# Block-sparse attention and a hard-swish MLP in one kernel: the turning of the attention's output moved from TensorE to VectorE, with batch 0's first product in four parts

## The chip, the cores and the metric

One core of a Trainium2 chip runs the whole program. The metric is the device time of one execution in microseconds (us); the kernel before takes 340.51 us, the median of three runs (339.76 to 341.34).

## What is computed

Eight batches, eight heads, 32 global and 512 local tokens, head size 64. Global tokens attend to everything; local tokens attend to the global ones and to a band of 32 tokens to each side. The result, 4352 rows of 512, goes through a two-layer MLP with a hard-swish between.

```python
k_all = np.concatenate([k_g, k_l], axis=2); v_all = np.concatenate([v_g, v_l], axis=2)
out_g = sm(scale * q_g @ k_all^T) @ v_all
s_ll = np.where(abs(i - j) <= 32, scale * q_l @ k_l^T, -1e9)
out_l = sm(concat(scale * q_l @ k_g^T, s_ll)) @ concat(v_g, v_l)
x = concat(out_g, out_l).transpose(0, 2, 1, 3).reshape(4352, 512)
h = x @ w_in                      # 512 -> 2048
out = (h * np.clip(h + 3, 0, 6) / 6) @ w_out
```

## The kernel before

**Who sets the order.** The kernel does not emit instructions as it goes. It builds operations (`Op`) with an engine and a cost, puts them on named streams with ranks (L286), and `Plan.lay` (L118) lays them out on a clock of its own: at each step the operation that can start first, among those within 0.03 us the one of lowest rank. Operations that ScalarE (ACT) or VectorE (DVE) can do (`either`, L303, and a few others) go to the one that would end first, with `SPARE` added on DVE's side. Buffers (`Buf`) are claimed in the plan and freed at their last reader. What comes out is a fixed order of instructions for each engine; real waits come from the data. The planner's costs are its own, and no time in this text comes from them.

**Attention of a batch.** The 512 local tokens of a batch are 16 units of 32; unit i of the first half and unit i of the second half (f = 0, 1) are worked on together, and two such i make a pair, so four pairs (`local`, L603). A pair goes through scores on PE into the two s banks (L624 or, for batches 0 and 1, L637; in batch 0 every second pair takes m banks), masked maximum on DVE (L664), exponential on ACT (L670), turning on PE (L679), copy of the turned weights to `et` on ACT or DVE (L308, L310), values on PE into `a` (L693), and normalising on DVE (reciprocal L701, product L702) into `x`. Then `x`, which has tokens on partitions, has to be turned so that the model dimension lies on partitions: four 128x128 turns on PE into PSUM (L715) and a copy to `xt` (stream "xpc", L308 or L310). The global tokens (`globe`, L723, twice a batch) go the same way: scores L735 or L743, two maxima and their union (L751, L752), exponentials L757 and L758, turning L768, copy to `etg`, values L777, normalising L785 and L786, and one turn on PE (L792) with a copy to `xg`.

**MLP.** `moe_first` (L868) runs the first product in 16 groups (c), each four matmuls of 512 columns (L821) into one of three m banks; ACT makes min/relu's first half into `t` (L833), DVE multiplies (the gate, L828) into `gts`, and the m bank is free again. Batch 0 is done in two parts of 256 columns, so that it can start after two of the four pairs. `moe_second` (L885) takes 16 matmuls of 512 columns (L850) for each 128 tokens, also in m banks, then a copy to `ot` (L858 or L860) and one store from SyncE's queue (SP). The global tokens of all batches are done together near the end (`moe_global`, L891). The MLP of a batch runs on PE between the attention steps of the next; `hold` (L807) ties the attention of batch b to the progress of the first product of batch b − 1.

**Loads.** They go out on GpSimd's queue (POOL): q and k of batch 0, the global v, the four blocks of V (L470), then w_in in eight pieces, two halves of 1024 columns of four each (L498), of which at most three are on the way in the plan (`AHEAD`), then batch 1. A piece of w_in holds 64 partitions and two of the four 128-row blocks. Copies of the global v into the value tile `vs` ("spreads", L459) go out on SP, and the strips of local v are copied into `vs` by POOL, in batch 0 also by ACT and DVE (L484, L486). POOL also clears the second buffers (`clear`, L353).

Of the kernel before, what the change touches and what calls it, by code (L numbers as in the profile page):

```python
# [37 lines left out]
class Plan:  # L38
# [7 lines left out]
    SPARE, PHASES = 0.3, 9  # L46
# [137 lines left out]
def kernel(  # L184
# [13 lines left out]
    P = 128  # L198
# [19 lines left out]
    AHEAD = 3  # L218
# [23 lines left out]
    for c in range(NDFF):  # L242
        sizes[f"gts{c}"] = 2
# [42 lines left out]
    for name, rank in (("l0", 0), ("ld", 5), ("lq", -2), ("sh", 0), ("sq", 0), ("st", 2), ("g0", 0), ("ga", -9), ("first", -9), ("gc", -3), ("msk", 1), ("tq", lambda n: 0 if n < 5 else 3), ("kg", 0.5), ("vs", 1.5), ("clr", 1),  # L286
                       ("s", -1), ("mx", lambda n: 1.2 if n < 33 else 2.7), ("ex", 1.2), ("t", -0.5), ("etc", 0), ("av", 0), ("nm", 0),
                       ("xp", -1.2), ("xpc", 0), ("gx", 1), ("gxc", 1),
                       ("mf", lambda n: 9 + n * 1e-3), ("ms", lambda n: 9 + (n + 2 * NDFF + 2) * 1e-3), ("t1", 0), ("gate", -1.4), ("ot", 1.5)):
        plan.stream(name, rank)  # L290
# [161 lines left out]
    def vg_load(b, to):  # L452

        st = state[b]
        v = st["v"] = Buf("v", NI // 2 + 2)
# [3 lines left out]
        for u in (2, 3, 0, 1):  # L459
            a = ORDER[u].index("g") * W  # L460
            st["vs"][u, 0] = [load("sh", "SP", 0.5, 0.3, lambda u=u, a=a: vs[v.slot][a:a + W, u],
                                lambda: vg[v.slot][0:W].rearrange("p (j h) d -> p j h d", j=1).to_broadcast([W, NJ, H, D1]), [g], lat=2.0 + LATE[b])]
            st["vs"][u, 1] = list(st["vs"][u, 0])

    def v_loads(b, to):
# [7 lines left out]
        def shift(u, z, n, src, js, dj):  # L473
# [129 lines left out]
    def local(b, n, spare, halves=False):  # L603
# [8 lines left out]
        def scored(r):  # L612
            return mps[ps[r].slot] if spare else sps[r]
# [363 lines left out]
```

## Time and profile before

| | us |
|---|---|
| median of 3 runs (lowest, highest) | 340.51 (339.76, 341.34) |
| the profiled execution | 340.96 |
| its span, first to last instruction | 339.2 |
| TensorE clock granted, mean | 0.983 |
| ACT busy, of the span | 234.1 |
| POOL busy, of the span | 156.2 |

The profile page gives busy time by engine, the span in 40 slices with the busy share of each engine in tenths, the chain of work that ended last, followed back from the last instruction, and the costliest groups of instructions: line, engine, operation, output and inputs, count, then busy us, mean ns of one, and the idle time just before them with what ended it. PE is the matmul row of TensorE and PEld its weight loads. A timeline row gives start, length, engine, line and a count of merged instructions; the length of a matmul row holds the drain of its last matmul, so the price of a group on PE is read from the start of one row to the start of the next.

### The profile page before, as it was taken

How to read it: one execution, taken by the hardware profiler on the slowest of the kernel's cores; microseconds unless marked ns; L12 is line 12 of the kernel's file. 1: busy time of each engine (PE TensorE's matmuls, PEld its weight loads, DVE VectorE, ACT ScalarE, POOL GpSimd, SP SyncE). 2: the span in 40 equal slices, each digit the busy share in tenths (PEclk: the TensorE clock that was granted, in tenths of full speed). 3: DMA queues.
4: the chain of work that ended last, by engine and by line, in shares of the span. 5: the costliest groups of instructions: out<-in, count | busy, mean ns of one | idle time of the engine just before them, and what ended most of it. 6: DMA issues, size and time to landing. Idle time of an engine off the chain costs nothing.

```text
span 339.2 us, 11248 instructions
## 1 busy us (share of the span) xinstructions
PE 313.6 (92%) x4456; PEld 169.5 (50%) x4456; DVE 257.0 (76%) x952; ACT 234.1 (69%) x576; POOL 156.2 (46%) x195
## 2 busy tenths in 40 slices
PE   0648879899999999999999999999999999999996
PEld 0536656454455455544554555454545544445654
DVE  5887997678988799989998999899969844433310
ACT  4778778555888697679867784799699644443431
POOL 8899589108961982694359258756000000000000
PEclk9976999999999999999999999999999999999999
DMA  8989999979960996999679948991000000010103
GB/s 131 185 154 165 185 227 164 177 204 147 221 124 35 154 206 86 91 153 179 145 99 150 169 90 80 183 174 41 31 33 34 35 32 33 31 60 34 62 34 92
DMA packets 107076, 39.27 MB, mean 116 GB/s; under 512 B 92368, under 2 KB 100816, under 8 KB 107024
## 3 DMA queue, kind: packets, MB, share of 16 engines
q0 software_dynamic: 93536, 17.44, 64.6%
q1 hardware_dynamic: 12912, 20.99, 22.7%
q8 instruction: 35, 0.57, 0.7%
q10 hardware_dynamic: 576, 0.13, 0.2%
q14 instruction: 17, 0.14, 0.1%
HBM read 35.39 MB, written 8.91 MB: 131 GB/s over the span
## 4 chain that ended last, share of the span: by engine, by line
PE 87%; DVE 7%; issue 2%; POOL 1%; ACT 1%; POOLq 0%; ACTq 0%
PE m L850 36%; PE m L821 33%; PE t L679 5%; PE a L693 3%; PE s L624 2%; PE t L715 2%; DVE gts L828 1%; PE t L768 1%; PE s L735 1%; PE s L637 1%; PE a L777 1%; DVE sm L664 1%; POOL wout L298 1%; DVE kt L534 1%; DVE qt L529 1%
## 5 line engine op out<-in xcount | busy, mean ns | idle before, releaser
L850 PE MATMUL m<-wout,gts 128*128 128x512 f16 (+1 forms) x560 | 135.1, 373 | 0.0
L828 DVE SCALAR_TENSOR_TENSOR gts<-t,m 128x512 f16<-128x512 f32 (+1 forms) x160 | 95.2, 602 | 46.1 <-ACT t L833 45.0
L821 PE MATMUL m<-xt,win 128*128 128x512 f16 (+1 forms) x576 | 126.9, 359 | 3.0 <-DVE gts L828 1.9
L833 ACT ACTIVATE t<-m 128x512 f32<-128x512 f32 (+1 forms) x160 | 84.3, 532 | 44.6 <-PE m L821 41.2
L486 POOL COPY vs<-v 32x1056 f32<-32x1056 f32 (+3 forms) x81 | 78.2, 966 | 34.9 <-DMA v<-in_v_l_dram 30.1
L670 ACT ACTIVATE ex<-sm,mx 128x128 f16<-128x128 f32 x256 | 86.1, 394 | 8.4 <-DVE mx L664 7.9
L821 PEld LDWEIGHTS <-win 128*128 128x128 f16 x640 | 59.9, 99 | 54.3 <-issue 4.2
L850 PEld LDWEIGHTS <-gts 128*128 128x128 f16 x560 | 51.1, 98 | 48.5 <-issue 0.7
L664 DVE CUSTOM_DVE_ANT_0 sm<-s,mask 128x128 f32<-128x128 f32 x240 | 56.9, 285 | 5.9 <-PE s L624 2.9
L858 ACT COPY ot<-m 128x512 f32<-128x512 f32 (+1 forms) x34 | 19.5, 573 | 16.9 <-PE m L850 16.2
L298 POOL DMA_DIRECT2D rawq<-in_q_l_dram x12 | 12.6, 1057 | 36.2 <-DMA vs<-vg 16.3
L298 POOL DMA_DIRECT2D v<-in_v_l_dram x32 | 28.2, 905 | 0.0
L702 DVE TENSOR_TENSOR x<-a,rec 128x512 f16<-128x512 f32 x32 | 22.1, 692 | 1.1
L664 DVE DVE_READ_ACCUMULATOR2_ANT mx<- 128x1 f32 x256 | 21.3, 83 | 0.0
L679 PE MATMUL t<-ident,ex 128*128 128x128 f16 x256 | 20.9, 228 | 0.0
L679 PEld LDWEIGHTS <-ex 128*128 128x128 f16 x256 | 17.2, 102 | 5.5 <-issue 0.7
L637 PE MATMUL s<-kt,qt 32*32 32x128 f16 x384 | 7.0, 246 | 12.3 <-DVE kt L542 10.0
L571 DVE STREAM_TRANSPOSE qt<-rawq 128x512 f16<-128x512 f16 x24 | 15.9, 692 | 0.0
L575 DVE STREAM_TRANSPOSE kt<-rawk 128x512 f16<-128x512 f16 x24 | 15.8, 687 | 0.0
L308 ACT COPY et<-t 128x1024 f16<-128x1024 f16 x13 | 13.1, 1010 | 3.5 <-PE t L679 3.4
L637 PEld LDWEIGHTS <-qt 32*32 32x32 f16 x512 | 6.5, 102 | 17.7 <-issue 9.6
L310 DVE COPY et<-t 128x1024 f16<-128x1024 f16 x19 | 13.0, 685 | 3.0 <-PE a L693 2.6
(95 smaller groups left out, 262.7 us busy)
## 6 DMA issues: line engine op xcount, KB each, us to landing
out_dram<-ot SPq DMA_DIRECT2D x31, 256.0 KB, 2.1
vs<-vg SPq DMA_DIRECT2D x32, 132.0 KB, 5.8
v<-in_v_l_dram POOLq DMA_DIRECT2D x32, 128.0 KB, 6.5
rawq<-in_q_l_dram POOLq DMA_DIRECT2D x12, 256.0 KB, 5.8
rawk<-in_k_l_dram POOLq DMA_DIRECT2D x12, 256.0 KB, 7.2
rawq<-rawq SPq DMA_DIRECT2D x12, 254.0 KB, 5.6
rawk<-rawk SPq DMA_DIRECT2D x12, 254.0 KB, 5.7
win<-in_moe_w_in_dram POOLq DMA_DIRECT2D x8, 256.0 KB, 6.2
```

What stands on the lines that cost most here:

```text
L298: eng.dma_start(out=o() if callable(o) else o, in_=i() if callable(i) else i)
L486: (nc.gpsimd if op.engine == "POOL" else nc.vector).tensor_copy(out=o(), in_=i())
L637: nc.tensor.matmul(out=scored(r)[quarter(e ^ r, f), z:z + P], lhsT=pairs(qt[k.slot])[rows, c, i * W:(i + 1) * W, bb], rhs=pairs(kt[k.slot] ...
L664: nc.vector.tensor_tensor_reduce(out=sms[sm.slot], in0=scored(c // 2)[:, z:z + P], in1=masks[:, m, :], scale=-scale, scalar=3.0e38, op0=AL ...
L670: nc.scalar.activation(out=exs[ex.slot][:, un, c, :], in_=sms[sm.slot], func=EXP, scale=-1.0, bias=mxs[mx.slot])
L679: nc.tensor.matmul(out=turned(tp)[:, z:z + P], lhsT=exs[ex.slot][:, un, c, :], rhs=ident, is_transpose=True)
L702: nc.vector.tensor_tensor(out=xs[x.slot], in0=o[:, :, :, 0:D], in1=recs[rec.slot].to_broadcast([P, 2, NC, D]), op=ALU.mult)
L821: nc.tensor.matmul(out=o if len(x.shape) == 2 else o.rearrange("p (a c) -> p a c", a=2), lhsT=w_in_t[c // 8][:, m, (c % 8) * P:(c % 8 + 1) ...
L828: nc.vector.scalar_tensor_tensor(out=g, in0=shape(t1s[t1.slot][:, 0:n]), scalar=1.0, in1=shape(mps[ps.slot][:, 0:n]), op0=ALU.min, op1=ALU ...
L833: r = plan.add("t1", Op(("ACT", 0.09 + n * 0.00083), lambda: nc.scalar.activation(out=t1s[t1.slot][:, 0:n], in_=mps[ps.slot][:, 0:n], func ...
L850: nc.tensor.matmul(out=mps[ps.slot][:, 0:n], lhsT=gfn(c), rhs=w_out_t[c // 4][:, c % 4, cols], start=(c == 0), stop=(c == NDFF - 1))
L858: nc.scalar.copy(out=o, in_=i)
```

## The change

- `x` is turned by DVE: one instruction turns the sixteen 32x32 blocks of a 128-partition stretch in place and writes them to `xt`. So that 32x32 blocks are enough, the values are laid out another way: the four quarters of the partitions of `a` hold four heads and not two heads by two halves, so that a block's 32 columns are 32 of the 64 numbers of a head. The PE turn and the copy from PSUM go. Rows of w_in are loaded in the order that matches (four blocks of 32 rows to 128 partitions for each of the four m).
- The tokens in `xt` stand pair by pair, 128 columns a pair. So batch 0's first product can be done in four parts, a pair each, in the order 1, 0, 2, 3; four groups c share an m bank, one ACT instruction and one gate. The global tokens share two groups a bank. A stretch of 128 tokens in `gts` is now two stretches of 64 rows of the output, so a store becomes two.
- The global rows: both halves' values are one operation, with one normalising, and a turn on DVE; the two s banks are one tile, and one instruction takes the maximum over both.
- The planner: other ranks, `SPARE` 0.8 for 0.3, `AHEAD` 4 for 3, the first w_in load behind V's second block, and two of batch 0's four spreads behind V's third.

```diff
-    SPARE, PHASES = 0.3, 9
+    SPARE, PHASES = 0.8, 9
...
-    AHEAD = 3
+    AHEAD = 4
+    PARTS, CG = 4, 4
...
-    gts = [tiles(f"gts{r}_", NDFF, [P, Sl], FP16) for r in range(2)]
+    gts = [tiles(f"gts{r}_", NDFF // CG, [P, CG, Sl], FP16) for r in range(2)]
-    sps = tiles("s", 2, [P, 512], FP32, pp)
+    sps = tiles("s", 1, [P, 2, 512], FP32, pp)[0]
...
-                       ("s", -1), ..., ("ex", 1.2), ("t", -0.5), ("etc", 0), ("av", 0), ("nm", 0),
-                       ("xp", -1.2), ("xpc", 0), ("gx", 1), ("gxc", 1),
+                       ("s", -1), ..., ("ex", 1.2), ("t", -0.5), ("etc", -0.7), ("av", -1.5), ("nm", -1.5),
+                       ("xp", -0.5), ("gx", 1),
...
-        for u in (2, 3, 0, 1):
+        spread(b, (2, 3, 0, 1) if b else (2, 3), g)
...
+        if b == 0:
+            spread(b, (0, 1), vl[NJ - 2])
...
-        rows = moe_w_in.rearrange("(k a e d) c -> a k d e c", k=2, a=2, e=2)
+        rows = moe_w_in.rearrange("(k h a d) c -> k a h d c", k=2, h=4, a=2)
...
-                    got.append(load("l0", "POOL", 0.65, 1.4, w_in_t[i][a * D:(a + 1) * D, 2 * k:2 * k + 2],
-                                    rows[a, k, :, :, i * n:(i + 1) * n], got[-AHEAD:][:1] if len(got) >= AHEAD else ()))
+                    got.append(load("l0", "POOL", 0.65, 1.4, w_in_t[i][:, 2 * k + a], rows[k, a, :, :, i * n:(i + 1) * n],
+                                    got[-AHEAD:][:1] if len(got) >= AHEAD else state[0]["v0"][1:2] if not got else ()))
...
-                for c in range(NC):
-                    for e in range(2):
-                        for f in range(2):
-                            nc.tensor.matmul(out=o[quarter(e, f), un, c, 0:D + 1],
+                for f in range(2):
+                    for kh in range(2):
+                        for hq in range(4):
+                            h = 4 * kh + hq
+                            c, e = h // 2, h % 2
+                            nc.tensor.matmul(out=o[hq * W:(hq + 1) * W, f, 2 * un + kh, 0:D + 1],
...
         def xturn():
-            o = turned(xp)[:, 0:4 * P].rearrange("d (k z n q) -> d k z n q", k=2, z=NU, n=2)
-            for un in range(2):
-                for kk in range(2):
-                    nc.tensor.matmul(out=o[:, kk, :, un, :], lhsT=xs[x.slot][:, un, 2 * kk:2 * kk + 2].rearrange("p a d -> p (a d)"),
-                                     rhs=ident, is_transpose=True)
-        a = plan.add("xp", Op(("PE", 0.24), xturn, done, [xp], [x], lat=0.25, n=8))
-        st["xT", n] = either("xpc", ...)
+            nc.vector.transpose(out=xts[xt.slot][:, :, n * P:(n + 1) * P].rearrange("p k (t q) -> p t k q", q=W),
+                                in_=xs[x.slot].rearrange("p f (u k) (a q) -> p (f u) (k a) q", u=2, a=2))
+        st["xT", n] = plan.add("xp", Op(("DVE", 0.7), xturn, done, new, [x]))
...
-            for f in range(2):
-                nc.vector.tensor_reduce(out=tops[mx.slot][:, f:f + 1], in_=sps[f][:, 0:N1]..., axis=AX, op=ALU.max)
+            nc.vector.tensor_reduce(out=tops[mx.slot][:, 0:1], in_=sps[:, :, 0:N1], axis=AX, op=ALU.max)
...
+        a = plan.add("av", Op(("PE", 0.48), lambda: [f(av) for f, _, _ in both], ...))
+        st["xg"] = plan.add("gx", Op(("DVE", 0.22), lambda: nc.vector.transpose(
+            out=xg[:, :, b * Sg:(b + 1) * Sg], in_=xgns[xgn.slot].rearrange("p k (a q) -> p (k a) q", q=W)), [n], (), [xgn]))
...
-        parts = 2 if b == 0 else 1
+        parts = PARTS if b == 0 else 1
+        for at, h in enumerate((1, 0, 2, 3) if parts == 4 else range(parts)):
+            for c in range(0, NDFF, parts):
+                cs = range(c, c + parts)
...
-               [(out[row:row + P, :], 0, P)], parts)
+               [(rows[f, j * P // 2:(j + 1) * P // 2], f * P // 2, P // 2) for f in range(2)], parts)
```

More of the change, by code (lines that the diff above doesn't have):

```diff
@@ L241 @@
              "eg": 2, "etg": 2, "xgn": 2, "t1": 3, "ot": 3, "m": 3, "t": 1, "s": 1, "a": 1, "mx": 16, "rec": 4}
-    for c in range(NDFF):
+    for c in range(NDFF // CG):
         sizes[f"gts{c}"] = 2
@@ L741, in scores @@
                     for cc, e, z in four:
-                        rows, c = quarter(e, f), 2 * cc + s
-                        nc.tensor.matmul(out=sps[f][z, 0:N1], lhsT=pairs(qg[k.slot])[rows, c, :, bb],
+                        rows, c = quarter(e, f), 2 * cc + of(cc)
+                        nc.tensor.matmul(out=sps[z, f, 0:N1], lhsT=pairs(qg[k.slot])[rows, c, :, bb],
                                          rhs=pairs(kt[k.slot])[rows, c, 2 * W:2 * W + N1, bb], start=(bb == 0), stop=(bb == 1))
@@ L784, in normal @@
[L784 to L796 removed]
+                    q = 2 * of(cc) + e
@@ L899, in moe_global @@
         for i in range(B // per):
-            second(lambda c, i=i: gts[gb[c].slot][c][:, i * P:(i + 1) * P], lambda c: [gb[c]], lambda c: [gd[c]],
+            second(lambda c, i=i: gts[gb[c].slot][c // CG][:, c % CG, i * P:(i + 1) * P], lambda c: [gb[c]], lambda c: [gd[c]],
                    [(rows[i * per + b, 0:Sg, :], b * Sg, Sg) for b in range(per)])
@@ L934 @@
                 globe(b, s)
+            globe_values(b)
         for b in range(B):
             moe_first(b)
-            for j in range(NJ - (b == B - 1)):
+            for j in ((1, 0, 2, 3) if b == 0 and PARTS == 4 else range(NJ - (b == B - 1))):
                 moe_second(b, j)
```

135 lines of the change are left out of this document (68 added, 67 removed).

## The prediction

> **What bounds the kernel now.** I read the page's busy shares and slices first, then its chain of work that ended last.
>
> ```profile
> span 339.2 us, 11248 instructions
> PE 313.6 (92%) x4456; PEld 169.5 (50%) x4456; DVE 257.0 (76%) x952; ACT 234.1 (69%) x576; POOL 156.2 (46%) x195
> ...
> PE   0648879899999999999999999999999999999996
> ...
> DVE  5887997678988799989998999899969844433310
> ...
> PE 87%; DVE 7%; issue 2%; POOL 1%; ACT 1%; POOLq 0%; ACTq 0%
> ```
>
> The reader is to see three stages. In slices 1 to 8 of 8.5 us PE has holes and DVE has 5 to 9 tenths; from slice 9 PE is full almost to the end; DVE has 9 tenths in most slices up to the 31st and falls off from the 33rd. A busy PE is a modelled PE, so the second look is at stretches, at PE's waits and at the chain inside the full stretch (three answers below: busy time by stretch; PE's waits from 21 to 76 us, then the same question for 76 to 330 us, which has its heading and no row; the chain from 76 to 326 us).
>
> ```profile
> 21.00:48.50 27.50, 21.62 (x391) 15.79 (x380) 24.30 (x92) 20.93 (x60) 22.31 (x30) 0.82 1.25 180
> 76.00:270.00 194.00, 194.00 (x2868) 98.36 (x2867) 176.42 (x665) 153.69 (x370) 103.95 (x111) 1.00 0.97 117
> ...
> PE m L821 <- DVE gts L828: 1.9, 2, 1.4
> ...
> engine line waited for: us in total, times, longest us
> ...
> by line: PE m L821 41.9%; PE m L850 39.7%; PE t L679 4.6%; PE a L693 3.4%; PE s L624 3.3%; PE t L715 2.2%; PE s L735 1.7%; PE t L768 1.5%; PE a L777 1.4%; PE t L792 0.2%; issue 0.0%
> ```
>
> In a stretch the columns after its length are the busy us of PE, PEld, DVE, ACT, POOL. From 76 to 326 us the chain is PE alone and PE waits for nobody: there, PE work taken away is time taken away, as long as DVE (176.4 of 194 us, 91%) and ACT (79%) still keep ahead. From 21 to 48.5 us DVE is busy 24.3 of 27.5 us and PE 21.6: there DVE sets the pace, and PE work there is nearly free.
>
> **The change part by part.**
>
> **The turning of x on PE, L715 and L792, goes.** PE's timeline gives its price as displacement, start to start, not as busy time:
>
> ```profile
> 67.80 0.40 PE L715 MATMUL t<-ident,x 128*128 128x128 f16 x4
> ...
> 73.14 0.39 PE L715 MATMUL t<-ident,x 128*128 128x128 f16 x4
> ...
> 121.87 0.61 PE L679 MATMUL t<-ident,ex 128*128 128x128 f16 x8
> 122.32 1.89 PE L821 MATMUL m<-xt,win 128*128 128x512 f16 x8
> 124.14 0.43 PE L693 MATMUL a<-vs,et 128*32 128x65 f16 x32
> ...
> 124.85 1.90 PE L821 MATMUL m<-xt,win 128*128 128x512 f16 x8
> 126.58 0.39 PE L715 MATMUL t<-ident,x 128*128 128x128 f16 x4
> 126.81 1.89 PE L821 MATMUL m<-xt,win 128*128 128x512 f16 x8
> ...
> 150.28 0.22 PE L792 MATMUL t<-ident,xgn 128*128 128x128 f16 x1
> 150.34 1.89 PE L821 MATMUL m<-xt,win 128*128 128x512 f16 x8
> ```
>
> A pair's turn takes 126.81 − 126.58 = 0.23 us of PE. The chain says the same: 2.2% of 250 us is 5.5 us for the 24 pairs of batches 2 to 7. With batch 1's four (67.8 to 73.5 us, PE full too) it is 28 × 0.23 = 6.4 us. Batch 0's four lie where DVE rules; I take nothing for them. The global rows' turn is 150.34 − 150.28 = 0.06 us, 8 times: 0.5 us.
>
> **The two value sums of the global rows become one.** One change of PE's array shape fewer per batch. Its price is the hole ahead of a group of that shape: eight products of 512 columns take 126.58 − 124.85 = 1.73 us, those at 122.32 are done at 124.05, and the value group starts at 124.14, so 0.09 us; eight of them, 0.7 us. Bounds 0 and 8 × 0.43 (the busy time of a whole value group) = 3.4 us; I take the hole, since all 80 matmuls stay.
>
> **DVE and ACT exchange work.** DVE gets 32 block transposes of 128x512 and 8 of 128x128. In the order that the planner lays out for the changed kernel it loses 18 of 19 copies of et, all 11 of xt, both of etg and xg, and its gates and maxima come in fewer, longer instructions. Rows of the groups by shape:
>
> ```profile
> L571 DVE STREAM_TRANSPOSE qt<-rawq 128x512 f16<-128x512 f16 x24 | 15.9, 692 | 0.0
> L578 DVE STREAM_TRANSPOSE qg<-gn 128x128 f16<-128x128 f16 x6 | 1.7, 284 | 0.0
> L310 DVE COPY et<-t 128x1024 f16<-128x1024 f16 x19 | 13.0, 685 | 3.0 <-PE a L693 2.6 <-PE t L679 0.2
> L310 DVE COPY xt<-t 128x512 f16<-128x512 f16 x11 | 4.6, 423 | 3.0 <-PE t L715 2.9
> L828 DVE SCALAR_TENSOR_TENSOR gts<-t,m 128x512 f16<-128x512 f32 x112 | 76.2, 682 | 30.4 <-ACT t L833 29.5
> L828 DVE SCALAR_TENSOR_TENSOR gts<-t,m 128x256 f16<-128x256 f32 x48 | 19.0, 416 | 15.8 <-ACT t L833 15.4
> L751 DVE TENSOR_REDUCE top<-s 128x1 f32<-128x288 f32 x32 | 12.9, 445 | 0.9 <-PE s L735 0.9
> L786 DVE TENSOR_TENSOR xgn<-a,rec 128x64 f16<-128x64 f32 x16 | 3.6, 225 | 0.6
> L308 ACT COPY et<-t 128x1024 f16<-128x1024 f16 x13 | 13.1, 1010 | 3.5 <-PE t L679 3.4
> L308 ACT COPY xt<-t 128x512 f16<-128x512 f16 x19 | 11.1, 582 | 6.2 <-PE t L715 6.1
> L833 ACT ACTIVATE t<-m 128x512 f32<-128x512 f32 x112 | 66.6, 595 | 30.3 <-PE m L821 27.7 <-PE t L715 0.8 <-DVE gts L828 0.7
> L833 ACT ACTIVATE t<-m 128x256 f32<-128x256 f32 x48 | 17.7, 384 | 14.3 <-PE m L821 13.6 <-DVE xgn L786 0.2
> ```
>
> DVE gains 32 × 0.69 + 8 × 0.28 = 24.4 us. It loses 18 × 0.685 + 11 × 0.42 = 17.0 us of copies; 48 × 0.416 − 24 × 0.682 = 3.6 us of gates; 2.3 us of maxima (32 of 288 columns become 16 of 576, at 0.445 + 288 × (0.682 − 0.416)/256 = 0.74 us each, 14.2 − 11.9); and half of L786, 1.8 us: 24.7 us, the few copies of etg and xg not counted. So DVE stays as it is. ACT loses 21 × 0.58 = 12.2 us of xt and 48 × 0.384 − 24 × 0.595 = 4.2 us of L833 and gains 18 × 1.01 = 18.2 us of et: 2 us more. The PE-bound stretch shrinks from 194 to about 187 us: DVE goes from 91 to about 94% there, ACT from 79 to some 84%. I cost the exchange at nothing; the cover is that slack, and the second and third rivals are its loss. The bound downward is nothing too, since PE already waits for neither.
>
> **Batch 0's first product in four parts.** 128 matmuls of 256 columns become 256 of 128 columns, each with a weight load of its own. Eight turns of 128 columns, also with a load each, take 122.32 − 121.87 = 0.45 us, 56 ns each; eight of 512 take the 1.73 us, so 108 ns for 256 columns. Hence 256 × 56 − 128 × 108 ns = +0.5 us, which I take. Bounds: 0 (pure columns), and 256 × 99 − 128 × 108 ns = +11.5 us if each waited out its weight load (the L821 PEld row below); the eight turns speak against that end. By the Trainium skill (TensorE: Matmul & The Clock Gate, section "Back-to-back issue gap") a sustained stream of loads and 128-column matmuls runs at about 81 ns each, which would make it +6.9 us; this trace's 56 ns does not agree.
>
> **The start.** The first product can begin when one pair is turned, not two, and the four loads of w_in's first half are issued together, after the clearing that used to follow them on POOL, 12.51 to 15.83 us, 3.3 us.
>
> ```profile
> 27.75 2.72 PE L821 MATMUL m<-xt,win 128*128 128x256 f16 x12
> ...
> 10.75 1.83 POOL L298 DMA_DIRECT2D win<-in_moe_w_in_dram  x3
> 12.51 0.62 POOL L354 MEMSET vg<- 128x528 f16 x1
> ...
> 15.30 0.53 POOL L361 MEMSET vs<- 32x528 f16 x1
> ...
> 20.52 0.59 POOL L298 DMA_DIRECT2D win<-in_moe_w_in_dram  x1
> ...
> win<-in_moe_w_in_dram POOLq DMA_DIRECT2D x1, 256.0 KB, 3.7
> ...
> L821 PEld LDWEIGHTS <-win 128*128 128x128 f16 x640 | 59.9, 99 | 54.3 <-issue 4.2
> ...
> 61.24 0.38 SPq L298 DMA_DIRECT2D out_dram<-ot  x1
> ```
>
> Issued from 10.75 + 3.3 = 14.1 us on, about 0.6 us each, they are out by 16.5 us, where the fourth used to go out at 20.5 and land 3.7 us later at 24.2. So the first product should start near 24 to 25 us, not 27.75. That is not the gain, because DVE rules until 48.5 us. In the new order DVE has, up to batch 1's first maxima, two copies of et and one of xt less, four transposes more, and 12 gates of 512 in place of 20 of 256: 4 × 0.69 + 12 × 0.682 − 2 × 0.685 − 0.42 − 20 × 0.416 = 0.8 us more, but 24 half-size gates' worth done in place of 20, which are 4 × 0.416 = 1.7 us ahead: 0.9 us gained. DVE's idle time, 27.5 − 24.3 = 3.2 us, may shrink besides, between nothing and all of it; of that I take a third, since the products now come in more and earlier pieces. Below nothing: the next half of w_in is the first rival. I take 2.0 us, bounds −2.6 and 4.1. That w_in waits for V's second block and two spreads for its third moves only the planner's clock: SP's queue begins in the same order as before, so nothing for it.
>
> **The stores** become two of 64 rows in place of one of 128. An issue takes SP 0.38 us (61.24 us); SP has long gaps, and what is queued behind, the spreads and the doubled q and k of the next batches, is needed a batch later. Only the last part's second issue is on the path: −0.3 us, between 0 and −0.4. The changed ranks and the V buffer's earlier release only shape the order counted above.
>
> Sum: 6.4 + 0.5 + 0.7 + 2.0 − 0.5 − 0.3 = 8.8 us off the profiled execution's own 340.96 us (its span 339.2 and 1.8 around it): 332.2. That execution is 0.4 us over the median of 340.51, so I say 332.0.
>
> **The rivals.**
> - **w_in's second half comes late.** Its loads follow six V copies on POOL, at about 21 to 24 us, and the new order has its first use as the third group of the first quarter, at about 28 us, with the global rows' scores behind it on PE (in the kernel before it was the ninth group). A load's form changes from 64 rows of two pieces to four blocks of 32 rows. If that form spread over a quarter of the DMA engines, the 3.7 us alone would become up to 14.8; halfway, about 9, the last lands near 33, PE stands 5 us, DVE's own work covers half of it, and the start loses 2.6 in place of gaining 2.0: 336.8. For it: four loads at once hide such a form, one after another does not. Against: no row shows a load spread less. The Trainium skill (DMA: Bandwidth & Descriptors, section "Why a DMA increments its semaphore by 16 and not by 1") has a rule of this kind: the number of engines is the largest up to 16 that divides the slowest dimension of both sides, here 4; no run here shows it yet.
> - **PE's freed time turns into waits on DVE at 94%.** Then only the start and the small terms remain: 340.96 − 2 = 339. For it: the 9 tenths of DVE in most slices; against it: PE waited for nothing in those.
> - **Slower: the three m banks.** Place: L821's groups, which need a bank back from L833 and L828. While two other groups run (2 × 0.86 = 1.7 us), 0.595 + 0.682 and some 0.1 of gaps must pass: 0.35 us to spare. An et copy of 1.01 us on ACT ahead of L833 overshoots by 0.66 us; the 18 copies that move there would cost 11.9 us: 332.2 + 11.9 = 344. It decides from about 9 us, where it eats the gain, so from three quarters of the copies standing there. Against: 13 et and 19 xt copies are on ACT now and PE waits for none; and second-product groups lie between for half the time.
> - **Better:** every term at its good bound: 4.1 for the start, nothing for the 128-column products and the stores, 3.4 for the value groups: 332.2 − 2.1 − 0.8 − 2.7 = 326.6.
>
> **How the numbers follow.** Forecast 332 (328.5 to 335) 0.62; late w_in 0.14; waits on DVE 0.09; slower 0.09; better 0.06. The range 327 to 338 holds the forecast and late w_in, and leaves out the slower case, most of the waits on DVE and the far end of the better one. About 0.5%, 1.7 us, is what a measurement of this kernel can tell from no change: faster 0.62 + 0.14 + 0.06 and a third of the waits on DVE, 0.85; within it the other two thirds, 0.06; slower 0.09.
>
> **What would show it.** PE's waits from 76 us on still empty, no L715 or L792 rows, and the first product's groups 0.23 us closer together; DVE's total within 5 us of 257 and ACT's of 234; new transposes near 0.69 us; 16 matmuls of 128 columns about 0.9 us apart; the first product near 24 to 25 us. Wrong if PE shows waits on L828 or L833 in the full stretch, if w_in's loads land 8 us or more after issue, or if the 128-column groups take over 1.2 us.

## The result, and the profile after

| | before | after |
|---|---|---|
| median of the runs (16 and 16, same chip) | 340.93 us | 336.91 us |
| lowest to highest | 339.44 to 342.04 | 336.20 to 340.17 |
| profiled execution, its span | 340.96, 339.2 | 336.76, 335.0 |

The ratio is 0.9893, 95% interval 0.9876 to 0.9909: faster by 4.0 us, 1.1%. The forecast was 332.0, which is 8.5 us under the 340.51 known then, so less than half of the forecast gain came; the time itself lies at the first rival's 336.8. Of the experiments below, one execution each of e7_spare03 and e8_old_order was slow and is left out, which lowers their medians by 0.3 us.

Busy shares, three of the slice rows and the summary of the chain, from the page of the kernel after:

```profile
span 335.0 us, 11129 instructions
PE 306.6 (92%) x4448; PEld 164.8 (49%) x4448; DVE 255.5 (76%) x902; ACT 239.2 (71%) x548; POOL 155.7 (46%) x193
...
PE   0547978899999999999999999999999999999994
...
DVE  5886697678878988998998899889988986442210
...
PE 85%; POOL 4%; DVE 3%; DMA 3%; issue 2%; ACT 1%; POOLq 0%; ACTq 0%
```

PE lost 7.0 us of busy time (313.6 to 306.6). DVE's total stayed (257.0 to 255.5) and ACT's grew by 5.1. New in the chain is DMA with 3%, one piece of 11 us.

The steady part, by the busy time of one stretch (after its length: PE, PEld, DVE, ACT, POOL), by PE's waits from 76 to 330 us (the heading has no row under it) and by the chain from 76 to 326 us:

```profile
76.00:270.00 194.00, 193.90 (x2734) 94.51 (x2732) 175.67 (x642) 158.58 (x362) 104.17 (x111) 1.00 1.03 121
...
engine line waited for: us in total, times, longest us
...
by line: PE m L828 42.6%; PE m L855 41.1%; PE t L688 4.3%; PE a L705 3.4%; PE s L633 3.4%; PE s L742 1.6%; PE t L773 1.4%; PE a L783 1.2%; DVE top L757 0.3%; DVE xt L725 0.3%; issue 0.3%; DVE rec L713 0.1%; DVE x L714 0.0%; DVE mx L758 0.0%
```

PE is still the bound and waits for nobody, and L715 and L792 are gone from its chain. The chain now touches DVE for 0.7%, some 1.7 us, most of it near 112 us; in two of the experiments PE waits for DVE just behind that place. To see what that is worth, the kernel is cut at two instructions that both versions have: batch 1's first product of 512 columns, and ACT's last copy, which starts as PE ends. From the timelines of PE and ACT (start, length, what), first before:

```profile
74.87 1.89 PE L821 MATMUL m<-xt,win 128*128 128x512 f16 x8
...
336.07 0.37 ACT L858 COPY ot<-m 128x256 f32<-128x256 f32 x1 [1.33 <-PE m L850]
```

and after:

```profile
75.81 1.89 PE L828 MATMUL m<-xt,win 128*128 128x512 f16 x8
...
330.53 0.37 ACT L863 COPY ot<-m 128x256 f32<-128x256 f32 x1 [1.37 <-PE m L855]
```

| stage | before | after | change | forecast |
|---|---|---|---|---|
| to batch 1's first 512-column product | 74.87 | 75.81 | +0.94 | 2.0 + 0.9 − 0.5 = 2.4 earlier |
| from there to ACT's last copy | 261.20 | 254.72 | −6.48 | 24 × 0.23 + 7 × (0.06 + 0.09) = 6.6 less |
| from there to the end of the span | 3.1 | 4.5 | +1.3 | +0.3 |

The steady part came as forecast to a tenth, which is in part luck: the steady parts of three other kernels with PE's old work (e2_before_newform, e9_before_order, e10_before_spare) took 260.1 to 261.2 us. Of the missing 4.6 us (8.8 forecast for this execution, 4.2 got) 3.4 are in the start and 1.0 in the tail.

In the start, rows from the timelines of PE and of its weight loads, and the loads' median from issue to landing, after:

```profile
25.48 0.51 PE L828 MATMUL m<-xt,win 128*128 128x128 f16 x2
26.45 3.03 PE L828 MATMUL m<-xt,win 128*128 128x128 f16 x26 [0.46 <-DMA win<-in_moe_w_in_dram]
...
33.50 0.64 PE L828 MATMUL m<-xt,win 128*128 128x128 f16 x4
...
33.90 0.10 PEld L828 LDWEIGHTS <-win 128*128 128x128 f16 x1 [0.25 <-DMA win<-in_moe_w_in_dram]
...
win<-in_moe_w_in_dram POOLq DMA_DIRECT2D x8, 256.0 KB, 10.6
```

The first product starts at 25.48 us, 2.3 earlier than before, and stops for 0.46 us after two matmuls, for w_in's first half. The third group, which needs w_in's second half, comes at 33.50, and its last weight load waits 0.25 us for it. PE's waits from 21 to 76 us hold no other wait for w_in. A load of w_in lands 10.6 us after its issue; before, the same row said 6.2. The chain from 21 to 50 us and POOL's timeline say what that held up:

```profile
by line: DMA win<-in_moe_w_in_dram 38.0%; PE m L828 23.8%; DVE gts L835 12.0%; DVE qt L538 6.8%; DVE kt L543 6.7%; ACT ex L679 5.4%; issue 3.7%; PE t L688 3.0%; DVE x L714 2.4%; PE t L773 2.2%; DVE xt L725 2.1%; PE s L750 2.1%; PE a L705 2.
...
15.38 11.02 DMA win<-in_moe_w_in_dram
...
29.56 0.87 POOL L299 DMA_DIRECT2D v<-in_v_l_dram  x1 [1.22 <-DMA win<-in_moe_w_in_dram]
32.24 0.87 POOL L299 DMA_DIRECT2D v<-in_v_l_dram  x1 [1.80 <-DMA win<-in_moe_w_in_dram]
33.60 0.87 POOL L299 DMA_DIRECT2D v<-in_v_l_dram  x1 [0.49 <-DMA win<-in_moe_w_in_dram]
```

The piece of 11 us is the load that completes w_in's first half, from its issue to its landing at 26.40. It stands on the chain because the products behind it start when it lands. And three of batch 1's four V loads wait on POOL, 3.5 us in all, each until a load of w_in has landed; before, the four went out in one run at 29.32.

In the tail, the last stores in SP's queue. Before:

```profile
336.47 0.35 SPq L298 DMA_DIRECT2D out_dram<-ot  x1
```

after:

```profile
330.74 1.87 SPq L299 DMA_DIRECT2D out_dram<-ot  x3
...
332.02 0.59 SPq L299 DMA_DIRECT2D out_dram<-ot  x1
```

Before, the last store went out at 336.47, as ACT's last copy ended (336.07 + 0.37). After, that copy ends at 330.90 and the last store goes out at 332.02: SP issues the last three back to back, 1.87 us for three, and the last one's data had been there for 1.1 us.

### The profile page after: what moved, and what is told of

It is laid out like the page before. It is cut to its first block, busy times and chain, and to the rows that moved or that the text cites. A ratio compares the mean times of both kernels' runs of the same rounds, so it can differ in the third digit from the quotient of the medians.

```text
span 335.0 us, 11129 instructions
## 1 busy us (share of the span) xinstructions
PE 306.6 (92%) x4448; PEld 164.8 (49%) x4448; DVE 255.5 (76%) x902; ACT 239.2 (71%) x548; POOL 155.7 (46%) x193
## 4 chain that ended last, share of the span: by engine, by line
PE 85%; POOL 4%; DVE 3%; DMA 3%; issue 2%; ACT 1%; POOLq 0%; ACTq 0%
PE m L855 35%; PE m L828 35%; PE t L688 4%; DMA win<-in_moe_w_in_dram 3%; PE a L705 3%; PE s L633 3%; PE t L773 1%; PE s L742 1%; POOL v L299 1%; DVE gts L835 1%; PE s L646 1%; POOL wout L299 1%; PE a L783 1%; DVE qt L538 1%; DVE kt L543 1%
## 5 line engine op out<-in xcount | busy, mean ns | idle before, releaser
L855 PE MATMUL m<-wout,gts 128*128 128x512 f16 (+1 forms) x560 | 132.1, 374 | 0.0
L828 PE MATMUL m<-xt,win 128*128 128x512 f16 (+1 forms) x704 | 124.9, 327 | 3.2 <-DVE gts L835 2.5
L835 DVE SCALAR_TENSOR_TENSOR gts<-t,m 128x512 f16<-128x512 f32 x136 | 91.7, 682 | 35.7 <-ACT t L839 34.2
L839 ACT ACTIVATE t<-m 128x512 f32<-128x512 f32 x136 | 80.9, 596 | 45.8 <-PE m L828 43.5
L828 PEld LDWEIGHTS <-win 128*128 128x128 f16 x768 | 65.2, 101 | 56.1 <-issue 4.6
L309 ACT COPY et<-t 128x1024 f16<-128x1024 f16 x29 | 29.3, 1009 | 7.3 <-PE t L688 7.2
L725 DVE STREAM_TRANSPOSE xt<-x 128x512 f16<-128x512 f16 x32 | 22.5, 704 | 0.2
L705 PEld LDWEIGHTS <-et 128*32 128x32 f16 x1024 | 10.2, 98 | 13.9 <-ACT ex L679 5.1
L309 ACT COPY etg<-t 128x640 f16<-128x640 f16 x16 | 11.1, 691 | 8.2 <-PE t L773 8.2
L705 PE MATMUL a<-vs,et 128*32 128x65 f16 x1024 | 14.4, 198 | 2.5 <-issue 1.2
## 6 DMA issues: line engine op xcount, KB each, us to landing
win<-in_moe_w_in_dram POOLq DMA_DIRECT2D x8, 256.0 KB, 10.6
```

The lines of the kernel that those rows point to most:

```text
L309: nc.scalar.copy(out=o(), in_=i())
L705: nc.tensor.matmul(out=o[hq * W:(hq + 1) * W, f, 2 * un + kh, 0:D + 1], lhsT=ets[et.slot][:, un, c, quarter(e, f) if b >= WORDS else quart ...
L725: nc.vector.transpose(out=xts[xt.slot][:, :, n * P:(n + 1) * P].rearrange("p k (t q) -> p t k q", q=W), in_=xs[x.slot].rearrange("p f (u k ...
L828: nc.tensor.matmul(out=mps[ps.slot][:, k * n:(k + 1) * n], lhsT=w_in_t[c // 8][:, m, (c % 8) * P:(c % 8 + 1) * P], rhs=x, start=(m == 0), ...
L835: nc.vector.scalar_tensor_tensor(out=g, in0=shape(t1s[t1.slot][:, 0:all_]), scalar=1.0, in1=shape(mps[ps.slot][:, 0:all_]), op0=ALU.min, o ...
L839: r = plan.add("t1", Op(("ACT", 0.09 + all_ * 0.00083), lambda: nc.scalar.activation(out=t1s[t1.slot][:, 0:all_], in_=mps[ps.slot][:, 0:al ...
```

## The experiments

Every kernel ran beside the kernel before on the same chip (medians of that: 341.06 us in the first and third group of runs, 341.2 in the second). Medians and ratios to it; the text compares medians, which the ratios bear out to within 0.9 us:

| run | us | ratio, 95% interval |
|---|---|---|
| e1_oldform | 334.20 | 0.9788 [0.9758, 0.9818] |
| e2_before_newform | 342.60 | 1.0042 [1.0017, 1.0068] |
| e3_parts2 | 338.47 | 0.9913 [0.9879, 0.9948] |
| e4_tail | 336.05 | 0.9850 [0.9817, 0.9882] |
| e5_heads | 334.53 | 0.9799 [0.9775, 0.9823] |
| e6_heads_tail | 333.96 | 0.9787 [0.9761, 0.9813] |
| e7_spare03 | 341.21 | 1.0006 [0.9982, 1.0031] |
| e8_old_order | 338.87 | 0.9929 [0.9905, 0.9953] |
| e9_before_order | 342.35 | 1.0032 [1.0004, 1.0059] |
| e10_before_spare | 344.38 | 1.0085 [1.0052, 1.0118] |
| e11_turns | 340.03 | 0.9958 [0.9932, 0.9984] |

**The loads' form, taken back in the kernel after.** The same eight loads of 256 KB in the same places of every queue, but in the form of the kernel before:

```diff
-        rows = moe_w_in.rearrange("(k h a d) c -> k a h d c", k=2, h=4, a=2)
+        rows = moe_w_in.rearrange("(k a e d) c -> a k d e c", k=2, a=2, e=2)
...
-   w_in_t[i][:, 2 * k + a], rows[k, a, :, :, i * n:(i + 1) * n]
+   w_in_t[i][a * D:(a + 1) * D, 2 * k:2 * k + 2], rows[a, k, :, :, i * n:(i + 1) * n]
```

> The changed kernel, with w_in's eight loads in the form of the kernel before (64 partitions, two blocks of rows each); the same places, sizes and order of every instruction. Rows of w_in then stand in an order that does not match x, so the output is another product; nothing else differs. Theory A (the start is lost to the loads' new form, which lands in 10.6 us in place of 6.2): landing falls to 7 us or less, the third group of the first product starts at 31 us or earlier in place of 33.5, and the time falls by 1.5 to 3 us below the changed kernel's 336.9, to some 334.5. Theory B (the start is lost to the order on PE and ACT and to PE's half clock): landing may fall, the time stays within 0.7 us of 336.9.

334.20 us, 2.7 under the kernel after; its slowest execution (334.82) lies under the fastest of the kernel after (336.20). PE's timeline and the landing:

```profile
25.59 2.83 PE L828 MATMUL m<-xt,win 128*128 128x128 f16 x28
...
32.27 0.40 PE L828 MATMUL m<-xt,win 128*128 128x128 f16 x4
...
72.41 1.89 PE L828 MATMUL m<-xt,win 128*128 128x512 f16 x8
...
win<-in_moe_w_in_dram POOLq DMA_DIRECT2D x8, 256.0 KB, 6.0
```

The loads land in 6.0 us, the first 28 matmuls run without a stop, and batch 1's first product is at 72.41 us: 2.5 earlier than in the kernel before, against 2.4 forecast. Nothing but the form of the loads was changed, so the form costs the 2.7 us.

The stages of this pair overstate it, since PE's granted clock differs: from 34 to 38 us it was 0.57 in the kernel after and 1.00 here, and the same 16 short products took 1.84 us there (35.24 to 37.08) and 0.99 here (33.59 to 34.58). That theory B's clock is not the cause of the rest is shown by e5_heads below.

**The new form alone, in the kernel before.**

```diff
-        rows = moe_w_in.rearrange("(k a e d) c -> a k d e c", k=2, a=2, e=2)
+        rows = moe_w_in.rearrange("(k h a d) c -> k a h d c", k=2, h=4, a=2)
```

> The kernel before, with w_in's eight loads in the changed kernel's form (128 partitions in four blocks of 32 rows), three on the way as before. Rows of w_in then do not match x, so the output is another product. Theory A: landing rises from 6.2 to about 10 us, the first product starts at 29 us or later in place of 27.75, and the time rises by 1 to 4 us. Theory B: within 0.7 us of the kernel before.

342.60 us, 1.5 over the kernel before. The landing goes from 6.2 to 10.2 us and the first product from 27.75 to 30.57, 2.8 later; by batch 1's first 512-column product 0.8 of it is left (75.68 against 74.87). So the new form costs time in both kernels, here about half of what it costs in the kernel after. Why the kernel after is hit harder was not tried apart; that it needs w_in's second half in the third group and not in the ninth can be little of it, since only the 0.25 us above were waited for.

**Two parts in place of four.**

```diff
-    PARTS, CG = 4, 4
+    PARTS, CG = 2, 4
```

> The changed kernel with batch 0's first product in two parts of 256 columns again (two groups a bank), all else as changed; the planner lays out a somewhat other order at the start. Theory C (in four parts, the first product's matmuls run at PE's half clock ahead of the turning of pair 2 and push pairs 2 and 3 back): turning of pair 2 moves from 29.3 to about 27 us and the time falls by 1 to 2 us. Theory A: the loads still land late, the time stays within 0.7 us or rises, since a first product of 256 columns must wait for two pairs.

338.47 us, 1.6 over the kernel after, though the intervals of the two ratios overlap. The first product comes at 28.61 us instead of 25.48, after a wait of 0.89 us for the second pair's turning. Theory A holds: the short matmuls were not what the kernel after lost, and the four parts are worth something between nothing and 1.5 us.

**Every second store of the tail from ACT.**

```diff
-            for o, p0, rows in stores:
-                load("st", "SP", 0.4, ...)
+            for at, (o, p0, rows) in enumerate(stores):
+                late = at % 2 and (parts == 2 or len(stores) == 4)
+                load("sa" if late else "st", "ACT" if late else "SP", 0.4, ...)
```

> The changed kernel with every second store of the global rows and of the last two half tiles issued from ACT's queue, which is nearly idle there, in place of SP's. Theory D (the doubled stores queue up on SP at the end: the last one goes out at 332.0 us where its data are ready at 330.9): the end comes 0.8 to 1.3 us earlier, 335.8, and the last landing is 3.2 us or less after PE's end in place of 4.5. Rival: the store's landing itself got longer, then less than 0.4 us changes.

336.05 us, 0.9 under the kernel after; as with the two parts, the intervals overlap, so the stage has to decide. From ACT's timeline:

```profile
330.38 0.37 ACT L863 COPY ot<-m 128x256 f32<-128x256 f32 x1 [0.66 <-PE m L855]
330.78 0.50 ACTq L299 DMA_DIRECT2D out_dram<-ot  x1
```

The last store goes out at 330.78, right behind its copy, and the span ends 3.6 us after that copy's start (334.0 − 330.38) where the kernel after took 4.5. The start (75.89) and the steady part (254.49) are within 0.3 us of those of the kernel after, so the whole gain is in the tail: the queue of doubled stores costs 0.9.

**A layout in which the old loads' kind of form fits.** The change puts head 4·half + group on row group `group`, so that a load of 128 rows is four blocks of 32 rows. With head 2·group + half, 32 partitions take four blocks each, and the product is the same:

```diff
-                            h = 4 * kh + hq
+                            h = 2 * hq + kh
...
-        rows = moe_w_in.rearrange("(k h a d) c -> k a h d c", k=2, h=4, a=2)
+        rows = moe_w_in.rearrange("(h m d) c -> h d m c", h=4, m=4)
...
+   w_in_t[i][h * W:(h + 1) * W], rows[h, :, :, i * n:(i + 1) * n]
```

The value sums of the global rows follow (row group 2·cc + (s^cc), column half e). e6_heads_tail has the stores of e4_tail besides.

> The changed kernel with heads laid out two by two over the row groups (head 2*group+column half in place of 4*half+group), so that w_in's loads can be 32 partitions of four blocks instead of 128 partitions of one, with the same output as the reference and the same order of all instructions. Theory A (the form of w_in's loads alone makes the start late): loads land in 6.0 to 6.6 us (after: 10.6), the first 512-column product of batch 1 at 72.4 to 73.2 us (after: 75.8), time 333.8 to 335.0, as with the loads of the kernel before. Rival (what counted there was the number of partitions, 64 against 128, and 32 is no better): landing 9 to 11 us, time 336 to 337. Rival (the new order of the values of the global rows costs something): at most 8 x 0.2 us above that, 335 to 336.

> The kernel of e5_heads with every second store of the last products and of the global rows issued by ACT. If the start's loss and the tail's loss are independent: e5's time less 0.9, so 332.9 to 334.1, faster than both kernels by 2% and 0.8%. Rival (an earlier end of PE makes the last stores bunch up anew, or ACT is the later one now): within 0.3 of e5_heads.

334.53 and 333.96 us. Rows of e5_heads, then the product of e6_heads_tail:

```profile
73.28 1.89 PE L827 MATMUL m<-xt,win 128*128 128x512 f16 x8
...
328.59 0.37 ACT L862 COPY ot<-m 128x256 f32<-128x256 f32 x1 [1.37 <-PE m L854]
...
win<-in_moe_w_in_dram POOLq DMA_DIRECT2D x8, 256.0 KB, 6.0
```

```profile
74.85 1.89 PE L827 MATMUL m<-xt,win 128*128 128x512 f16 x8
```

Theory A holds on landing and time. 32 partitions are no slower than 64, so a load does not lose by having few of them. What the two quick forms share is a first dimension of 64 or of 32 rows, where the slow one has the four blocks first and 128 partitions; which of these two decides was not tried apart.

The clock of this execution was like that of the kernel after: 0.50 from 22 to 30 us in both, 0.64 and 0.57 from 34 to 38. So here the 2.5 us between the two at batch 1's first 512-column product (73.28 against 75.81) are not the clock's. At a stretch of 36 short products still in batch 0 there are 1.2 of them (46.10 against 47.34); most of the rest is one wait of 1.2 us of a value matmul of the kernel after, at 66 us, for which the profile names no releaser.

e6_heads_tail beats both kernels: 2.1% under the one before and 0.9% under the one after. Its 0.6 us under e5_heads lie inside the intervals of the two, but its tail again takes 3.5 us where that of e5_heads takes 4.5. Its start, in which PE, DVE and ACT have the same instructions in the same order as in e5_heads, came out 1.6 us later (74.85). So one profiled start tells nothing finer than about 1.6 us: with the quick forms batch 1's product came between 0 and 2.5 us earlier than in the kernel before.

**The planner's margin as before, in the kernel after.**

```diff
-    SPARE, PHASES = 0.8, 9
+    SPARE, PHASES = 0.3, 9
```

> The changed kernel with the planner's spare margin back at 0.3, which puts more of the turned-probability copies on ACT and fewer on DVE. Theory (the steady part is PE alone: 254.7 us from batch 1's first 512-column product to PE's end): that stretch stays at 254.2 to 255.2 and the time at 336.3 to 337.5. Rival (DVE, which now turns the outputs, is near enough to the bound that who copies matters): over 338, with waits of PE on DVE or ACT after 76 us.

The expectation has the exchange the wrong way round: at 0.3 DVE makes 10 copies of et and ACT 22, in the kernel after 1 and 31. The time is 341.21, 4.3 over the kernel after, and the rival holds. From the page, PE's waits from 76 to 326 us, and the two timelines:

```profile
PE 309.0 (91%) x4448; PEld 165.8 (49%) x4448; DVE 263.0 (78%) x916; ACT 230.6 (68%) x534; POOL 156.1 (46%) x193
...
PE m L828 <- DVE xt L725: 1.8, 1, 1.8
PE a L705 <- POOL vs L493: 0.5, 1, 0.5
PE m L855 <- DVE gts L835: 0.2, 1, 0.2
...
77.68 1.90 PE L828 MATMUL m<-xt,win 128*128 128x512 f16 x8
...
334.99 0.37 ACT L863 COPY ot<-m 128x256 f32<-128x256 f32 x1 [1.38 <-PE m L855]
```

DVE has 7.5 us more, and now PE waits, 2.5 us, most of it once, for a turned output, at 117 us. The steady part takes 257.31 us, 2.6 more, and the start is 1.9 later. That the copies on DVE are what makes PE wait is not shown by this alone: the next experiment has the same steady part with no such copy on DVE.

**The old order of the first loads, on e5_heads.** Three loads on the way, none behind V's second block, all four spreads at once:

```diff
-    AHEAD = 4
+    AHEAD = 3
...
-   got[-AHEAD:][:1] if len(got) >= AHEAD else state[0]["v0"][1:2] if not got else ()
+   got[-AHEAD:][:1] if len(got) >= AHEAD else ()
...
-        spread(b, (2, 3, 0, 1) if b else (2, 3), g)
+        spread(b, (2, 3, 0, 1), g)
```

> The kernel of e5_heads with the loads issued as before the change: w_in's first load not behind V's second block, three on the way, all four spreads of V's global rows at once. Theory A (only the form was at fault, the new order is worth little): within 0.8 us of e5_heads, 333.4 to 335.8. Theory B (the new order is what makes the start early): the first transposed outputs of batch 0 come 1 to 3 us later, because V's blocks land later behind w_in, and the time is 335.5 to 337.5. Rival (the new order only delays w_in): first 512-column product of batch 1 up to 1.5 us earlier, time 332.5 to 333.8.

338.87 us, 4.3 over e5_heads and outside all three expectations. (The profiled execution, 341.19, is 2 us above the median, so its stages overstate.) From PE's timeline, the loads, and PE's waits from 76 to 326 us:

```profile
23.43 10.19 DMA win<-in_moe_w_in_dram
...
33.66 0.61 PE L825 MATMUL m<-xt,win 128*128 128x128 f16 x4 [0.33 <-DMA win<-in_moe_w_in_dram]
...
76.95 1.89 PE L825 MATMUL m<-xt,win 128*128 128x512 f16 x8
...
win<-in_moe_w_in_dram POOLq DMA_DIRECT2D x8, 256.0 KB, 8.9
...
PE m L825 <- DVE xt L722: 0.9, 1, 0.9
PE m L825 <- DVE gts L832: 0.7, 1, 0.7
...
334.26 0.37 ACT L860 COPY ot<-m 128x256 f32<-128x256 f32 x1 [1.37 <-PE m L852]
```

Even in the good form w_in's second half is late now: its last load is out at 23.43 us on the chain and lands 10.19 us later, and batch 1's first product is 3.7 us behind e5_heads. Of these, 1.9 are there before w_in is used: scores start at 20.87 us after a wait of 3.6 us without a named releaser, and at 18.95 after 1.8 in e5_heads. The steady part, 257.31 us, is 2.0 longer than there, with 1.6 us of waits for DVE, though the margin is 0.8 and all 32 copies of et are on ACT. So the new order, which I had costed at nothing ("moves only the planner's clock"), is worth about 4 us to the kernel with four parts, in the start and behind it.

**The new order alone, in the kernel before** (the edit above, the other way round).

> The kernel before with only the new order of the first loads: w_in's first load behind V's second block, four on the way, two of the spreads behind V's third block; its loads keep their own form. Theory (the order is worth its 4.6 us between e5_heads and e8_old_order only together with the early first quarter of batch 0): within 1 us of the kernel before, 340.2 to 342.2. Rival (the order is worth something by itself, because V's blocks no longer queue behind w_in): first product 1 to 3 us earlier than 27.75 us, time 337.5 to 340.

342.35 us, 1.3 over the kernel before. The first product is at 27.36 in place of 27.75 us and batch 1's at 75.51 in place of 74.87. So the order gains nothing by itself. Which part of the change it needs beside it to pay was not tried apart.

**The new margin alone, in the kernel before.**

```diff
-    SPARE, PHASES = 0.3, 9
+    SPARE, PHASES = 0.8, 9
```

> The kernel before with only the planner's spare margin at 0.8 in place of 0.3. Theory (in the kernel before PE is the bound from 76 us on and waits for nobody, so who copies is worth nothing there, and the margin only pays once DVE turns the outputs): 339.8 to 342.5. Rival (the margin by itself is a part of the change's gain): 336 to 339.

344.38 us, 3.3 slower: both expectations missed. By the timelines the steady part is no worse,

```profile
78.09 1.04 PE L821 MATMUL m<-xt,win 128*128 128x512 f16 x4
...
338.35 0.37 ACT L858 COPY ot<-m 128x256 f32<-128x256 f32 x1 [1.33 <-PE m L850]
```

260.26 us against 261.20; the whole loss is the start, 3.2 us, where the first product comes at 31.71. Ahead of that product PE waits 2.8 us for ACT, for exponentials and for two copies of et; in the kernel before such a copy was made by DVE there, and PE waited 0.3 us for it. So the margin, which moves copies to ACT, loses alone, and undoing it in the kernel after loses too; which part of the change makes it pay was not tried apart.

**PE's turns put back as dead work, on e5_heads.** Two of each pair's four blocks are turned twice into the same place, four more turns in each pair of batches 1 to 7:

```diff
-                for c in range(NC):
+                for c in tuple(range(NC)) + ((0, 1) if b else ()):
```

> The kernel of e5_heads with four more turns of 128x128 on PE in each pair of batches 1 to 7: two of every pair's four probability blocks are turned twice into the same place, as many turns as the kernel before spent on its outputs; the output stays the same. Theory (PE is the bound there, and 28 pairs' turns are worth 28 x 0.23 = 6.4 us): 6.4 us over e5_heads, 340.0 to 341.8, and the stretch from batch 1's first 512-column product to PE's end 6 to 7 us longer than e5_heads. Rival (part of PE's freed time was no gain, because gaps between its groups would have covered it): under 4 us over e5_heads, 335.5 to 338.5.

340.03 us, 5.5 over e5_heads, at the lower edge of what the theory said.

```profile
95.70 0.83 PE L687 MATMUL t<-ident,ex 128*128 128x128 f16 x12
96.37 1.03 PE L854 MATMUL m<-wout,gts 128*128 128x512 f16 x4
...
74.97 1.89 PE L827 MATMUL m<-xt,win 128*128 128x512 f16 x8
...
334.90 0.37 ACT L862 COPY ot<-m 128x256 f32<-128x256 f32 x1 [1.38 <-PE m L854]
```

Twelve turns displace 96.37 − 95.70 = 0.67 us, eight 0.45: 0.22 for four. The steady part is 259.93 us, 4.6 over e5_heads (24 pairs, 0.19 us each), and the start 1.7 later. The turns of a pair that PE need not make are thus worth some 5.5/28 = 0.20 us on the clock, nearly their whole displacement.

## Why the prediction was right and wrong

- **The turning of x on PE, 6.4 us; the global turn, 0.5; the shape change, 0.7.** Right in sum: 6.48 us in the steady part against 6.6. That the turns carry most of it is shown by e11_turns (5.5 us for 28 pairs against 6.4). The two small terms were not tested by themselves.
- **The exchange between DVE and ACT, nothing.** Right for the kernel after: transposes of 128x512 take 704 ns (0.69 forecast), DVE's total is 1.5 us off the 257 and ACT's 5.1 off the 234, just past the bound of 5. But the slack that the prediction named as the cover is thin: with the margin at 0.3 (e7_spare03), and with the old order of the loads (e8_old_order), PE waits for DVE, 2.5 and 1.6 us, and the steady part is 2.6 and 2.0 us longer. The prediction did not say that the planner's settings are what keeps the price at nothing.
- **128-column matmuls, +0.5 us.** Near, but the term is a small difference of two large numbers: 52 of them from 50.11 to 53.30 us are 61 ns each, against 56 taken, and 256 × 61 − 128 × 108 ns would be +1.8 us:

```profile
50.11 3.27 PE L828 MATMUL m<-xt,win 128*128 128x128 f16 x52
53.30 0.64 PE L646 MATMUL s<-kt,qt 32*32 32x128 f16 x52
```

  The Trainium skill (TensorE: Matmul & The Clock Gate, section "Back-to-back issue gap") gives about 81 ns; this stretch at a granted clock of 1.00 does not agree.
- **The start, "I take 2.0 us": the step that failed.** It failed at the wait for w_in. The prediction priced a load of the new form with the landing of an old one issued alone, 3.7 us, and gave the case that the form spreads less a chance of 0.14. The loads landed in 10.6 us ("wrong if w_in's loads land 8 us or more after issue" stood in the text), the one that completes the first half stands on the chain with 11 us, and the start lost 0.9 us at batch 1's product in place of gaining 2.4. With an old form the same kernel is 2.7 us faster (e1_oldform), and 2.4 with the layout that fits such a form (e5_heads). Even the old form has no one price: the first three loads of the kernel before, issued together at 10.75 us, took 9.4.
  Two things in this step were off apart from the form. The first product came at 25.48 us, in place of 24 to 25, but with quick loads it came at 25.25 to 25.67 (e1_oldform, e5_heads, e6_heads_tail), so it is not w_in that it starts behind; in e1_oldform the chain reaches it through ACT's exponentials and a copy of et. And the 2.4 us that e1_oldform confirms is the best of three executions with quick loads, which gained 2.5, 1.6 and 0.0.
  How a late load becomes 2.7 us is followed in part only. In the kernel after, 0.7 us are waits of PE and its weight loads for w_in, and POOL's queue with batch 1's V behind it slipped by 3.5 us. But in e4_tail, which has the same start, the chain from 21 to 50 us does not pass w_in at all, and batch 1's product comes at the same time (75.89). There PE stands 1.9 us ahead of the first product, in the middle of a group, and the profile names no releaser ("issue"). Such waits add up, from 21 to 76 us, to 2.9 to 4.3 us in the four kernels with the slow form and the new order (after, e3_parts2, e4_tail, e7_spare03) and to 1.9 to 3.0 in the four with a quick form and the new order (e1_oldform, e5_heads, e6_heads_tail, e11_turns). So a part of the cost seems to come as such waits; what PE waits for in them stays open.
  The Trainium skill (DMA: Bandwidth & Descriptors, section "Why a DMA increments its semaphore by 16 and not by 1") would split such a load over 4 engines and the two other forms over 16. The landings of the three forms, 10.6 against 6.0 and 6.0, go the way of that rule, by a factor of 1.8 and not 4; how many engines each load used is shown by no view here.
- **The order of the first loads, "nothing for it".** Wrong in working, hidden in the sum: undone it costs 4.3 us (e8_old_order). So it doesn't stand by itself: order and margin undone cost 4.3 us each (e8_old_order, e7_spare03), part of it in the start and part in the steady part, and alone in the kernel before they lose 1.3 and 3.3 us. The gain that the forecast put down to "one pair, not two" needs both of them.
- **The stores, −0.3 us, bounds 0 and −0.4.** Mis-sized: 1.3 in the profiles, and 0.9 came back when half of them went to ACT. Only the last part's second issue was counted. But twice the stores stand in that one queue, an issue there took 0.6 us and not 0.38, and the last one waits for two others ahead of it, not for its data.
- **The rivals.** Late w_in is what happened, 336.8 against 336.91, and the last load landed at about 33.9 us, as it said. But its mechanism was not this one: it had PE stand 5 us for the second half, and PE stood 0.25. Its own sum had 2.6 us lost in the start; measured are 0.94 at batch 1's first product with 0.9 gained there by the turns and 0.5 taken as lost by the short matmuls, so 1.3 lost, and the tail's 1.0 makes up most of the rest. Its agreement to a tenth is luck. Waits on DVE in the full stretch are not there in the kernel after; they came in e7_spare03 and e8_old_order. For an m bank PE waited nowhere in that stretch; in the start it waited 2.5 us for gates (1.9 before).

Put together: e6_heads_tail, which has a quick form and the split stores, is 7.2 us faster than the kernel before, of the 8.8 that were added up; the last 1.6 us are about what two profiled executions differ by and stay open.

## What to carry to other kernels

Price a load by a row of its own form: when a rewrite changes which dimension of a transfer comes first, its landing is an unknown, and if it feeds the start, that unknown is the first rival and not the third. Then look for a layout that gives the transfer its old kind of form; here it was a renumbering of heads. Stores that are doubled cost an issue each in the queue that ends the kernel, so count every issue that stands behind the last data, not the last pair alone. And a retuned planner setting or load order belongs to the change that it came with: undone one at a time, each cost about as much as the whole change had gained, and alone each was a loss.

## What was not expected of the hardware

- The same 256 KB in eight loads land in 6.0 us as 64 partitions of two blocks or 32 partitions of four, and in 10.2 to 11.3 us as four blocks of 32 partitions (e1_oldform and e5_heads; the kernel after, e2_before_newform and e3_parts2). The quick forms are not always quick: they took 8.9 us in e8_old_order and 8.0 in e10_before_spare, where other instructions stand around them. Every kernel with the slow form moves 3072 packets more in POOL's queue (first row the kernel after, second e1_oldform), 384 for each load, at 0.01 MB more; what these packets are was not followed:

```profile
q0 software_dynamic: 96608, 17.45, 66.2%
```

```profile
q0 software_dynamic: 93536, 17.44, 66.0%
```

  The issue on POOL is longer too: four loads take 2.73 us in the kernel after and 2.19 in e5_heads:

```profile
13.97 2.73 POOL L299 DMA_DIRECT2D win<-in_moe_w_in_dram  x4
```

```profile
14.01 2.19 POOL L299 DMA_DIRECT2D win<-in_moe_w_in_dram  x4
```

- PE's granted clock was 0.50 from 22 to 30 us in some profiled executions (before, after, e5_heads) and 1.00 in others (e2_before_newform, e3_parts2, e6_heads_tail). First products at 30.57 and 28.61 us, later than before's 27.75, are among those with the full clock, and the kernel after and e5_heads, with much the same clock, are 2.5 us apart at batch 1's product. So the clock alone does not explain the start, though where it is 0.50 the products are about half as fast: 26 of 128 columns took 2.82 us (26.45 to 29.27), 108 ns each, against 61 at 1.00.
